# Norm transposes of a two-layer transformer kernel: from TensorE to transposing DMAs on SyncE's queue

## The chip, the cores and the metric

The kernel runs on one core of a Trainium2 chip. The metric is the device time of one launch in microseconds (us). The kernel before takes 1613.98 us, the median of three runs (1613.9 to 1615.33).

## The reference

The input x has 2048 rows of 512 bf16 values. Two layers follow, with the same weights in both:

```python
x = x + _A_ref(_layernorm(x, axis=-1), A_wqkv, A_wo)   # attention, 32 heads of 16
x = x + _B_ref(_layernorm(x, axis=-1), B_w1, B_w2)     # relu MLP, 512 -> 1792 -> 512
x = x + _A_ref(_layernorm(x, axis=-1), A_wqkv, A_wo)
x = x + _B_ref(_layernorm(x, axis=-1), B_w1, B_w2)
```

`_A_ref` makes q, k and v by one matmul, takes the softmax of q k^T / 4 over all 2048 keys, multiplies by v and by wo. `_layernorm` subtracts the mean and divides by the root of the variance plus 1e-5. So there are four norms over all 2048 rows, and the result of each is multiplied from the right by a weight matrix. The matmul contracts over partitions, so each normalised block of 128 rows x 512 columns has to be transposed to 512 x 128 first.

## The kernel before, in words

**Attention.** Scores are made transposed, keys on partitions and 512 queries along the free dimension, one PSUM bank for one head and one block of 128 keys. There are 4096 such banks. They are worked in *slots* of three banks (the `while units` loop from line 1173): TensorE makes the scores of a slot into one of two three-bank tiles `ps_s` (line 1302), ScalarE takes the exponential of two or three of them in one instruction (line 1311), and TensorE multiplies by the values and adds up in the bank `ps_o` (line 901). Four heads share TensorE by its four row groups.

**Pairs.** In about every second slot one of the three banks is handed to VectorE, which makes the exponential by a short chain: `lin` from the scores (line 995), and then, for two such banks together, `step` and `cube` (lines 1036 to 1051). Two banks together are a *pair*. A slot with one bank on VectorE has a shorter ScalarE instruction.

**The planner.** The order of instructions on each engine is written by the Python code itself, under a manual schedule. It keeps two model clocks, `now_pe` and `now_dve`, and gives each piece of work a cost in ns. `mark(key, engine, lag)` (line 240) records when a result is expected; `at(deps, engine)` (line 243) tells when an engine may use it. VectorE's tasks are in `dve_q`, with "musts" ahead (lin, and the copies that free a bank). A pair is started (lines 1196 to 1220) when fewer than four are in flight, when VectorE's expected backlog is under `BACKLOG`, and when its chain is expected to end before its segment does. In layer 0 no more than one pair at a time is in flight until the last value block is there (`("v", 0, 15)`).

**The filler.** All other matmuls (q, k, v, the output projection, the MLP) are "groups" in the lists `urgent` and `work`. They go through one PSUM bank, `ps_f`, one group at a time: TensorE fills the bank, VectorE empties it (`put_evac`, `do_evac`), and the next group may begin. `fill_pe` (line 307) puts pieces of them between the scores, as many as the ration `owed` allows; `pace` (line 1272) sets the ration per slot, 3.0 units of 216 ns in the first segments of layer 0. `fill_pe` takes the first group whose inputs are expected in time. `run_until` forces what is needed at once.

**The norms.** `ln_rows` (line 524) queues four steps: statistics of each block of 128 rows on VectorE (line 465), the inverse root on VectorE and GpSimd (lines 473 to 503, `RSTD_LAG` 5000 ns), the normalised block `xn` on VectorE (`ln_apply`, line 505), and then, as filler, `ln_groups` (line 549): four TensorE transposes of 128x128 into `ps_f` (`ln_transpose`, line 513) and one VectorE copy into `xnT` (line 558). A norm covers four row blocks, or two for the last four chunks of layer 1. `xnbuf` has one buffer for each of the four row blocks, so the apply of the next norm waits for the transpose of the one before (key `xT`). The key `xnT` releases the k, v, q and MLP groups.

The trace shows 64 row blocks: 58 through `ln_groups`, four in the opening code (lines 1090 to 1095) and two in the closing code (lines 1403 to 1406). These six are written out by hand.

**SyncE's queue.** It carries, in program order, the input loads at the start, the weight loads of the MLP (`load_w1`, line 662: one 128 KB block for each 128 hidden columns, four buffers), the stores of the output (line 711), and for the softmax sums two small DMAs per head group: line 828 spreads 512 sums over partitions so that VectorE's reciprocal (line 847) is short, line 848 brings them back. GpSimd's queue then broadcasts them (line 850). The planner expects 3600 ns for line 828 (`C_LAG`).

Of the kernel before, what the change touches and what calls it, by code (L numbers as in the profile page):

```python
# [24 lines left out]
def kernel(  # L25
# [10 lines left out]
    nc = tc.nc  # L36
    P = 128
# [12 lines left out]
    QS = 512  # L50
    NQS = S // QS
    TPC = QS // P
# [26 lines left out]
    C_LAG, R_LAG, U_LAG = 3600.0, 10500.0, 3000.0  # L79
    VLAG = 1  # L80
    RSTD_LAG = 5000.0
    AHEAD = (8.0, 8.0)
    LATE = 0.0
    MID = 2
# [15 lines left out]
    def sb(shape, dt, name):  # L100
        return persist.tile(shape, dt, name=name)
# [32 lines left out]
    xnT = [sb([P, NDC, QS], BF16, f"xnT{j}") for j in range(NQS)]  # L134
# [19 lines left out]
    xnbuf = [sb([P, D], BF16, f"xn{n}") for n in range(TPC)]  # L154
# [47 lines left out]
    def bank():  # L202
        if ending[0]:
            bank_no[0] += 1
            return (ps_f[:], ps_s[0][:, 0, :], ps_s[1][:, 0, :])[bank_no[0] % 3]
        if not wide[0]:
            return ps_f[:]
        n = bank_no[0] % 7
        bank_no[0] += 1
        in_bank[0] = (2, 0) if n == 6 else (n // W, n % W)  # L210
        if n == 6:
            return ps_f[:]
        return ps_s[n // W][:, n % W, :]
# [26 lines left out]
    def mark(key, engine="dve", lag=0.0):  # L240
        made[key] = (engine, (now_pe if engine == "pe" else now_dve)[0] + lag)
# [30 lines left out]
    work = []  # L272
# [5 lines left out]
    def task(cost, fn, makes=(), deps=(), place=None):  # L278
        t = {"cost": cost, "fn": fn, "makes": makes, "deps": deps}
        dve_q.insert(len(dve_q) if place is None else place, t)  # L280
        maker.update({k: t for k in makes})

    def group(pieces, makes, deps):
        g = {"pieces": pieces, "makes": makes, "deps": deps}
        maker.update({k: g for k in makes})
        return g

    def put_evac(cost, fn):
        evac.append((cost, now_pe[0] + PE_TO_DVE, fn))
# [160 lines left out]
    def columns(l, j):  # L450

        tt, n = chunks[l, j]
        return tt // TPC, tt % TPC * P, n * P
# [4 lines left out]
    def ln_n(tag):  # L458
        return ln_seq.index(tag) % 2

    def ln_stats(tag, tt, i):
        if tag not in ln_seq:
            ln_seq.append(tag)
        st = stats[i % 2]
        nc.vector.bn_stats(out=st[:], in_=x_t[tt][:])  # L465
        nc.vector.bn_aggr(out=mv[ln_n(tag)][:, i, :], in_=st[:])
# [38 lines left out]
    def ln_apply(tag, tt, i):  # L505
        n = ln_n(tag)
        nc.vector.tensor_scalar(
            out=xnbuf[i][:], in0=x_t[tt][:],
            scalar1=mv[n][:, i, 0:1], scalar2=ya_[n][:, i : i + 1],
            op0=ALU.subtract, op1=ALU.mult,  # L510
        )

    def ln_transpose(tag, i, b=None, at_bank=None):
        pt = (bank() if b is None else b).bitcast(BF16)
        for c in range(NDC):
            ins = nc.tensor.transpose(
                pt[:, c * P : (c + 1) * P], xnbuf[i][:, c * P : (c + 1) * P], ident[:]
            )
            if wide[0]:
                uses(ins, in_bank[0] if b is None else at_bank)  # L520
        mark(("xT", tag, i), "pe")
        return pt[:, 0 : NDC * P].rearrange("p (c f) -> p c f", c=NDC)

    def ln_rows(tag, tt, n, i):

        if tag not in ln_seq:
            ln_seq.append(tag)
        at_tag = ln_seq.index(tag)
        prev = ln_seq[at_tag - 1]
        rows_of_prev = chunks[prev[1:]][1]  # L530
        before_that = ln_seq[at_tag - 2] if at_tag > 1 else None
        old = each(chunks[before_that[1:]][1], "xn", before_that) if at_tag > 1 else []
        if ("st", tag, i) not in made:
            task(830, lambda: ln_stats(tag, tt + i, i), [("st", tag, i)], old)
        if i == n - 1:

            def rstd():
                ln_rstd(tag, 0)
                ln_newton(tag)
                mark(("rs", tag, 3), lag=RSTD_LAG)  # L540

            task(500, rstd, [("rs", tag, 3)], each(n, "st", tag) + old)
            for k in range(n):
                task(
                    325, lambda k=k: ln_apply(tag, tt + k, k), [("xn", tag, k)],
                    [("xT", prev, k)] * (k < rows_of_prev) + [("rs", tag, 3)],
                )

    def ln_groups(tag, dst, at_column, n, war):
        groups = []  # L550
        for i in range(n):

            def piece(i=i):
                pt = ln_transpose(tag, i)

                def fin():
                    a = at_column + i * P
                    nc.vector.tensor_copy(out=dst[:, :, a : a + P], in_=pt)
                    mark(("xnT", tag, i))

                put_evac(342, fin)

            groups.append(
                group([(1.3, piece)], [("xT", tag, i), ("xnT", tag, i)], [("xn", tag, i)] + war)
            )
        return groups

    def each(n, *key):
        return [key + (i,) for i in range(n)]
# [73 lines left out]
    def o_group(l, j, i):  # L643
        tt, n = chunks[l, j]
        a = columns(l, j)[1] + i * P

        def fin(b):
            nc.vector.tensor_add(out=x_t[tt + i][:], in0=x_t[tt + i][:], in1=b)
            mark(("o", l, j, i))
            ln_rows(("ln2", l, j), tt, n, i)  # L650

        return mm_group(
            [(ot[t][:, a : a + P], wo[:, t // 2, :]) for t in range(NT)], fin,
            [("o", l, j, i)],
            [("ot", l, j, t, i) for t in range(NT)],
        )
# [76 lines left out]
    def rest_of_chunk(l, j):  # L733

        b = before(l, j)
        xj, a, w = columns(l, j)
        n = w // P
        war_h = each(chunks[b][1], "z", *b) if b else []
        work[0:0] = [o_group(l, j, i) for i in range(n)] + ln_groups(
            ("ln2", l, j), xnT[xj], a, n, []  # L740
        )
        gs = [h_group(l, j, ft, war_h) for ft in range(0, NF, QS // w)]
        gs += [z_group(l, j, i) for i in range((l, j) == (1, LAST - 1), n)]
        if l == 0:
            gs += ln_groups(("ln1", 1, j), xnT[j], 0, TPC, [])
            gs.append(k_group(1, 0, j))
            gs += [v_group(1, kb) for kb in range(j * TPC, (j + 1) * TPC)]
            gs += [k_group(1, T, j) for T in range(1, 4)]
        return gs
# [321 lines left out]
    tag = ("ln1", 0, 0)  # L1071
    idle_matmuls(18)
    for e in range(2):
        nc.vector.tensor_reduce(
            out=mask[e][:],
            in_=ident[:].rearrange("p (g e d) -> p e g d", g=4, e=2)[:, e],
# [3 lines left out]
            out=qmask[e][:], in0=mask[e][:], scalar1=SCALE * LOG2E * UNIT, scalar2=None,  # L1080
# [9 lines left out]
    for i in range(TPC):  # L1090
        pt = ln_transpose(tag, i)
# [27 lines left out]
    for j in range(1, NQS):  # L1119
        tag = ("ln1", 0, j)  # L1120
        for i in range(TPC):
            ln_rows(tag, j * TPC, TPC, i)
        work.extend(k_group(0, T, 0) for T in FIRST_K[j])
        work.extend(ln_groups(tag, xnT[j], 0, TPC, []))
        work.append(k_group(0, 0, j))
        work.extend(v_group(0, kb) for kb in range(j * TPC, (j + 1) * TPC))
        if j == 1:
            work.extend(k_group(0, T, 1) for T in range(1, MID))
# [44 lines left out]
    while units:  # L1173
# [6 lines left out]
        for (sg, kb, g), *_ in banked:  # L1180
            if sg["n"] not in seen:
                seen.add(sg["n"])
                n = sg["n"] + 1
# [86 lines left out]
        if first["l"] and first["early"]:  # L1270
            rest = sum(x[0][0]["early"] for x in itertools.islice(units, 400)) / W - 20.0
        pace = (
            3.0 if first["short"] and not first["l"] else max(todo / max(rest + (-8.0 if first["j"] == NQS - 1 and not first["l"] else AHEAD[first["l"]] if first["j"] < (LAST if first["l"] else NQS - 1) else -6.0), 6.0), 0.5)
        )
# [34 lines left out]
        while len(pend) == NE:  # L1309
            force_v()  # L1310
        ex = nc.scalar.activation(  # L1311
            out=eb[:, 0 : place[m]], in_=b[:, 0 : place[m]], func=ACTF.Exp,
# [34 lines left out]
    l, j = 1, LAST  # L1347
    tag = ("ln2", l, j)
    tt, n_rows = chunks[l, j]
    rows = range(n_rows)  # L1350
    _, at_column, width = columns(l, j)
# [7 lines left out]
    def at_bank(b):  # L1359
        n, w = b  # L1360
        return ps_s[n][:, w, :] if n < 2 else (ps_f, ps_o)[n - 2][:]
# [41 lines left out]
    for i in rows:  # L1403
        pt = ln_transpose(tag, i, at_bank(more[i]), more[i])
# [4 lines left out]
    for ft in range(NF + 1):  # L1409
        if ft < NF:  # L1410
            n = (l * NQS + j) * NF + ft
# [6 lines left out]
            if ft % 2:  # L1418
                out = nc.scalar.activation(out=ht[ft][:, at_column : at_column + width], in_=at_bank(b)[:, 0:width], func=ACTF.Relu)
            else:  # L1420
                out = nc.vector.tensor_scalar(
                    out=ht[ft][:, at_column : at_column + width], in0=at_bank(b)[:, 0:width],
                    scalar1=0.0, scalar2=None, op0=ALU.max,
                )
# [8 lines left out]
    for i in rows:  # L1433
# [3 lines left out]
            out=out_flat[(tt + i) * P : (tt + i + 1) * P, :], in_=x_t[tt + i][:]  # L1437
# [31 lines left out]
```

The softmax here doesn't subtract the row's maximum and nothing guards it: scores larger than these inputs give would overflow.

## Time and profile before

| what | value |
|---|---|
| time, median of 3 | 1613.98 us |
| span of the profiled execution | 1611.5 us |
| ScalarE busy | 1566.0 us, 97% |
| VectorE busy | 1496.8 us, 93% |
| TensorE busy (matmul records) | 1451.6 us, 90% |
| 16 DMA engines, SyncE's hardware queue | 7.1% of their time |
| chain that ended last | 78% ScalarE, line 1311 |

Busy time is the union of the records of an engine; records of consecutive instructions overlap a little, so the spacing of starts is shorter than the mean duration. TensorE's records are pipelined, and 90% busy there is no 90% of its peak. The chain that ended last is followed back from the last instruction: its shares tell which engine's work the end hangs on. The waits name the instruction that came last before an engine went on. Entries such as SPq are instructions of a DMA queue; they show when a DMA was issued, and not when it landed.

### The profile page before, as it was taken

How to read it: one execution, taken by the hardware profiler on the slowest of the kernel's cores; microseconds unless marked ns; L12 is line 12 of the kernel's file. 1: busy time of each engine (PE TensorE's matmuls, PEld its weight loads, DVE VectorE, ACT ScalarE, POOL GpSimd, SP SyncE). 2: the span in 40 equal slices, each digit the busy share in tenths (PEclk: the TensorE clock that was granted, in tenths of full speed). 3: DMA queues.
4: the chain of work that ended last, by engine and by line, in shares of the span. 5: the costliest groups of instructions: out<-in, count | busy, mean ns of one | idle time of the engine just before them, and what ended most of it. 6: DMA issues, size and time to landing. Idle time of an engine off the chain costs nothing.

```text
span 1611.5 us, 35252 instructions
## 1 busy us (share of the span) xinstructions
PE 1451.6 (90%) x14667; PEld 508.9 (32%) x14863; DVE 1496.8 (93%) x3007; ACT 1566.0 (97%) x1387; POOL 93.8 (6%) x279
## 2 busy tenths in 40 slices
PE   8888888999989999899998998888989999899997
PEld 3222222322222222222222222222333333344444
DVE  7669999999999999999898998999999999999994
ACT  6999999999999999999999999999999999999993
POOL 2000001001010011000100000001001010010100
PEclk9999999999999999999999999999999999999999
DMA  5000000210002100021000100000210111121223
GB/s 164 1 1 2 2 2 10 46 28 12 5 18 45 21 15 9 12 47 25 9 1 17 31 1 1 2 3 9 44 30 16 26 29 36 22 48 36 47 46 73
DMA packets 113889, 39.97 MB, mean 25 GB/s; under 512 B 103328, under 2 KB 111264, under 8 KB 113728
## 3 DMA queue, kind: packets, MB, share of 16 engines
q1 hardware_dynamic: 101696, 26.21, 7.1%
q0 software_dynamic: 10688, 10.18, 3.4%
q8 instruction: 116, 1.90, 0.5%
q10 hardware_dynamic: 1344, 1.31, 0.2%
q14 instruction: 45, 0.37, 0.1%
HBM read 24.38 MB, written 2.10 MB: 16 GB/s over the span
## 4 chain that ended last, share of the span: by engine, by line
ACT 78%; PE 11%; DVE 7%; issue 3%; DMA 1%; ACTq 0%; DVEq 0%
ACT e L1311 78%; PE ps_s L1302 4%; PE ps_o L901 3%; PE ps_f L434 3%; DVE lin L995 2%; DVE step L1036 1%; PE ps_s L1365 1%; DVE cube L1047 1%; DVE cube L1051 1%; DVE stats L465 0%; DVE ht L682 0%; DVE q L625 0%; DVE ot L836 0%; DVE x L708 0%; DMA c<-u 0%
## 5 line engine op out<-in xcount | busy, mean ns | idle before, releaser
L1311 ACT ACTIVATE e<-ps_s 128x1024 bf16<-128x1024 f32 (+1 forms) x1366 | 1554.8, 1367 | 6.6 <-PE ps_s L1302 4.7
L1302 PE MATMUL ps_s<-q,ktp 32*128 32x512 bf16 (+1 forms) x6060 | 601.2, 341 | 106.7 <-ACT e L1311 84.7
L901 PE MATMUL ps_o<-e,vaug 128*32 128x512 bf16 (+1 forms) x4284 | 494.7, 345 | 11.3 <-DVE u L823 4.8
L995 DVE TENSOR_SCALAR lin<-ps_s 128x512 int16<-128x512 f32 x662 | 452.6, 686 | 35.8 <-PE ps_s L1302 30.4
L1302 PEld LDWEIGHTS <-ktp 32*128 32x128 bf16 x6060 | 189.9, 91 | 504.5 <-issue 375.6
L1036 DVE TENSOR_SCALAR step<-lin 128x1024 int16<-128x1024 int16 x662 | 262.9, 420 | 3.3 <-PE ps_o L901 0.6
L901 PEld LDWEIGHTS <-vaug 128*32 128x32 bf16 x6004 | 161.5, 94 | 302.2 <-issue 291.5
L1047 DVE TENSOR_TENSOR cube<-step 128x1024 f16<-128x1024 bf16 x331 | 225.9, 685 | 2.7
L1051 DVE TENSOR_TENSOR cube<-cube,lin 128x1024 bf16<-128x1024 f16 x331 | 225.5, 682 | 0.0
L901 PE MATMUL ps_o<-step,vaug 128*32 128x512 bf16 (+1 forms) x836 | 143.2, 340 | 0.3 <-issue 0.3
L901 PE MATMUL ps_o<-cube,vthird 128*32 128x512 bf16 (+1 forms) x788 | 138.2, 337 | 0.6 <-issue 0.3
L901 PE MATMUL ps_o<-lin,vaug 128*32 128x512 bf16 (+1 forms) x836 | 127.4, 338 | 4.1 <-DVE u L823 2.8
L434 PE MATMUL ps_f<-xnT,w 128*128 128x512 bf16 (+1 forms) x446 | 116.9, 345 | 5.6 <-issue 2.5
L434 PE MATMUL ps_f<-w,ht 128*128 128x512 bf16 x334 | 104.8, 384 | 5.6 <-issue 4.3
L850 POOL DMA_DIRECT2D r<-u x52 | 37.5, 721 | 1165.9 <-DVE step L1036 424.3
L434 PE MATMUL ps_f<-xnT,wqkv 128*128 128x512 bf16 (+1 forms) x288 | 82.3, 359 | 6.4 <-issue 2.5
L682 DVE TENSOR_SCALAR ht<-ps_f 128x512 bf16<-128x512 f32 x103 | 70.7, 687 | 3.2 <-PE ps_f L434 3.0
L434 PE MATMUL ps_f<-wo,ot 128*128 128x512 bf16 x206 | 65.4, 384 | 3.0 <-issue 1.9
L625 DVE TENSOR_SCALAR q<-ps_f,qmask 128x512 bf16<-128x512 f32 (+1 forms) x102 | 64.8, 661 | 3.1 <-PE ps_f L434 3.0
L434 PEld LDWEIGHTS <-w 128*128 128x128 bf16 x504 | 39.1, 97 | 60.0 <-issue 50.6
L836 DVE SCALAR_TENSOR_TENSOR ot<-u,mask,r 128x512 bf16<-128x512 f32 (+2 forms) x82 | 51.3, 627 | 1.1
L901 PEld LDWEIGHTS <-vthird 128*32 128x32 bf16 x788 | 39.8, 95 | 32.8 <-issue 30.1
(91 smaller groups left out, 609.8 us busy)
## 6 DMA issues: line engine op xcount, KB each, us to landing
w<-in_B_w_dram SPq DMA_DIRECT2D x140, 128.0 KB
r<-u POOLq DMA_DIRECT2D x25, 256.0 KB, 7.1
r<-u POOLq DMA_DIRECT2D x27, 128.0 KB, 4.5
out_dram<-x SPq DMA_DIRECT2D x16, 128.0 KB
x<-in_A_x_dram SPq DMA_DIRECT2D x14, 128.0 KB
w<-in_B_w_dram SPq DMA_DIRECT2D x1, 1792.0 KB
wqkv<-in_A_wqkv_dram ACTq DMA_DIRECT2D x2, 512.0 KB
c<-u SPq DMA_DIRECT2D x48, 8.0 KB
```

Of the source, the lines that this page charges most:

```text
L434: nc.tensor.matmul(out, lhsT, rhs, start=i % k == 0, stop=i % k == k - 1)
L625: return nc.vector.tensor_scalar(out=qbuf[n % 2][e][:, 0:w], in0=b, scalar1=qmask[e][:, 0:1], scalar2=None, op0=ALU.mult,)
L682: nc.vector.tensor_scalar(out=out, in0=sums, scalar1=0.0, scalar2=None, op0=ALU.max)
L836: nc.vector.scalar_tensor_tensor(out=ot[t][:, at_column + a : at_column + a + w], in0=u[:, a : a + w], scalar=mask[e][:, 0:1], in1=r[:, a ...
L850: nc.gpsimd.dma_start(out=r[:, 0:width], in_=bass.AP(tensor=sums.tensor, offset=sums.offset, ap=[list(sums.ap[0]), [0, 32], [1, width]],),)
L901: nc.tensor.matmul(ps_o[32 * g : 32 * g + 32, 0 : sg["w"]], values[:, 4 * sg["T"] + g, 2 * e : 2 * e + 32], rhs, start=g not in sg["begun" ...
L995: first = nc.vector.tensor_scalar(out=lin[which][:, half * QS : (half + 1) * QS], in0=src, scalar1=EXP_BIAS, scalar2=0.0, op0=ALU.add, op1 ...
L1036: nc.vector.tensor_scalar(out=stair, in0=line, scalar1=keep, scalar2=put, op0=ALU.bitwise_and, op1=ALU.bitwise_or,)
L1047: (609, lambda: nc.vector.tensor_mul(out=power, in0=mantissa, in1=mantissa)),
L1051: (609, lambda: nc.vector.tensor_mul(out=power.bitcast(BF16), in0=power, in1=line.bitcast(BF16))),
L1302: nc.tensor.matmul(b[:, a : a + sg["w"]], kt[32 * g : 32 * g + 32, kc : kc + P], qbuf[sg["n"] % 2][sg["e"]][32 * g : 32 * g + 32, 0 : sg[" ...
L1311: ex = nc.scalar.activation(out=eb[:, 0 : place[m]], in_=b[:, 0 : place[m]], func=ACTF.Exp, scale=1.0 / (LOG2E * UNIT),)
```

## The change

In place of the filler groups, each apply of a norm is followed at once by a transposing DMA on SyncE's queue, from `xn` to its columns of `xnT`. The aim is to take the transposes off TensorE, the one filler bank out of the path, and the copy off VectorE. The planner is told that the transposed block is there 4000 ns after the apply (`X_LAG`); the same moment frees `xn` for the next norm. The opening four row blocks and the closing two stay on TensorE.

```diff
+    X_LAG = 4000.0
...
             task(500, rstd, [("rs", tag, 3)], each(n, "st", tag) + old)
+            def apply(k):
+                kind, l, j = tag
+                xj, a, _ = columns(l, j) if kind == "ln2" else (j, 0, QS)
+                ln_apply(tag, tt + k, k)
+                a += k * P
+                nc.sync.dma_start_transpose(out=xnT[xj][:, :, a : a + P], in_=xnbuf[k][:])
+                mark(("xT", tag, k), lag=X_LAG)
+                mark(("xnT", tag, k), lag=X_LAG)
+
             for k in range(n):
                 task(
-                    325, lambda k=k: ln_apply(tag, tt + k, k), [("xn", tag, k)],
+                    325, lambda k=k: apply(k),
+                    [("xn", tag, k), ("xT", tag, k), ("xnT", tag, k)],
                     [("xT", prev, k)] * (k < rows_of_prev) + [("rs", tag, 3)],
                 )
-
-    def ln_groups(tag, dst, at_column, n, war):
-        groups = []
-        for i in range(n):
-
-            def piece(i=i):
-                pt = ln_transpose(tag, i)
-
-                def fin():
-                    a = at_column + i * P
-                    nc.vector.tensor_copy(out=dst[:, :, a : a + P], in_=pt)
-                    mark(("xnT", tag, i))
-
-                put_evac(342, fin)
-
-            groups.append(
-                group([(1.3, piece)], [("xT", tag, i), ("xnT", tag, i)], [("xn", tag, i)] + war)
-            )
-        return groups
...
-        work[0:0] = [o_group(l, j, i) for i in range(n)] + ln_groups(
-            ("ln2", l, j), xnT[xj], a, n, []
-        )
+        work[0:0] = [o_group(l, j, i) for i in range(n)]
...
-            gs += ln_groups(("ln1", 1, j), xnT[j], 0, TPC, [])
...
-        work.extend(ln_groups(tag, xnT[j], 0, TPC, []))
```

## The prediction

> **What bounds the kernel now.** I read the busy shares and costliest groups of the page first, then the waits, then the timeline of one norm, then the DMA queue of SyncE.
>
> From the page, parts 1 and 5, and the groups kept apart by form:
>
> ```profile
> PE 1451.6 (90%) x14667; PEld 508.9 (32%) x14863; DVE 1496.8 (93%) x3007; ACT 1566.0 (97%) x1387; POOL 93.8 (6%) x279
> ...
> L1311 ACT ACTIVATE e<-ps_s 128x1536 bf16<-128x1536 f32 x703 | 1052.1, 1573 | 4.5 <-PE ps_s L1302 2.8 <-PE ps_o L901 1.2
> L1311 ACT ACTIVATE e<-ps_s 128x1024 bf16<-128x1024 f32 x662 | 717.7, 1148 | 2.1 <-PE ps_s L1302 1.9 <-PE ps_o L901 0.2
> L995 DVE TENSOR_SCALAR lin<-ps_s 128x512 int16<-128x512 f32 x662 | 452.6, 686 | 35.8 <-PE ps_s L1302 30.4
> ...
> L558 DVE COPY xnT<-ps_f 128x512 bf16<-128x512 bf16 x58 | 24.3, 419 | 3.6 <-PE ps_f L516 3.2
> L507 DVE TENSOR_SCALAR xn<-x,mv,ya 128x512 bf16<-128x512 bf16 x64 | 23.1, 409 | 0.8 <-POOL ya L503 0.7
> L516 PE MATMUL ps_f<-ident,xn 128*128 128x128 bf16 x232 | 22.8, 221 | 2.0 <-DVE q L625 0.6 <-DVE xnT L558 0.5
> ```
>
> ScalarE does nothing but exponentials from 16.8 us to about 1578 us and is idle ahead of them for 6.6 us in all. The end is therefore a head of 17 us, the sum of the exponentials, and a tail of 34 us. The 4096 score banks (2 layers, 32 heads, 16 key blocks, 4 query strips) come in slots of three: 703 slots give ScalarE all three banks, 662 give one to VectorE. A bank taken from ScalarE shortens a slot by 1573 - 1148 = 425 ns. So the time is set by how many pairs of banks the planner can place on VectorE (now 331), and by whether ScalarE is ever kept waiting.
>
> VectorE is the second engine, and it is full: the stretches of the trace give it 273 of 280 us from 120 to 400, 388 of 400 from 400 to 800, 183 of 200 from 800 to 1000, 193 of 200 from 1000 to 1200, 347 of 360 from 1200 to 1560. From 20 to 120 us it has only 70 of 100 us of work, with 15 banks (0.15 per us, against 135 in 280 us, 0.48 per us, just after), because pairs are withheld until the last value block of layer 0 is there.
>
> One norm of layer 0, VectorE's timeline from 225 to 300 us:
>
> ```profile
> 273.00 1.37 DVE L507 TENSOR_SCALAR xn<-x,mv,ya 128x512 bf16<-128x512 bf16 x4
> ...
> 276.09 0.42 DVE L558 COPY xnT<-ps_f 128x512 bf16<-128x512 bf16 x1
> ...
> 282.50 0.42 DVE L558 COPY xnT<-ps_f 128x512 bf16<-128x512 bf16 x1
> ...
> 285.98 0.69 DVE L682 TENSOR_SCALAR ht<-ps_f 128x512 bf16<-128x512 f32 x1
> ```
>
> The four normalised row blocks are there at 274.4; the four transposes and copies, one at a time through the one filler bank, last until 282.9; the first MLP matmul on them starts at 283.05. This path is 8.5 us long.
>
> SyncE's queue and GpSimd at the same place:
>
> ```profile
> 277.04 0.54 SPq L848 DMA_DIRECT2D u<-c  x1
> ...
> 279.36 0.70 POOL L850 DMA_DIRECT2D r<-u  x1 [7.24 <-DVE step L1036]
> ```
>
> The GpSimd DMA at line 850 needs the bytes of the SyncE DMA at line 848: 2.32 us from issue to dependent (2.38 at 252.79 to 255.17). That is the price of a small DMA from SyncE here: 0.54 us of issue, about 2.3 us until a waiter goes on.
>
> **What the Trainium skill says.** "VectorE: DVE Perf Modes", section "The three transpose paths", gives a 128x128 bf16 transpose 390 ns on TensorE and 1309 ns by the DMA crossbar. The TensorE record here is 221 ns, so the table is above this trace; no DMA transpose is in it. "DMA: Bandwidth & Descriptors", section "Latency and other measured facts", gives a transposing DMA an effective 261 GB/s; no run shows it yet. The same page, section "Silent corruption: two transposing streams in flight at once", asks for waits between transposes of different queues; all of these are SyncE's, so none is added.
>
> **The change, part by part.**
>
> *VectorE.* It loses the 58 copies of line 558. A record is 419 ns, but records overlap; by the starts (35.52 to 35.86) one takes 0.34 us of the stream. A pair costs, by the same reading, 2 x 0.60 (lin) + 2 x 0.34 (step) + 2 x 0.61 (cube) = 3.10 us, and saves ScalarE 2 x 0.425 = 0.85 us. Twelve of the copies lie in 20 to 120 us, where VectorE has idle time anyway. The other 46 free 46 x 0.34 = 15.6 us, so 5.0 pairs, so 4.3 us of ScalarE.
>
> *TensorE and the filler bank.* 232 transposes go. TensorE is not what ends the waits of ScalarE, so these 22.8 us are worth nothing as such. But the filler is rationed: in the first segments of layer 0 it gets 3.0 units a slot. Twelve row blocks x 1.3 = 15.6 units, 5.2 slots less until the last value block; at 80 slots in 100 us that is 6.5 us earlier. In 6.5 us the pairs run at 0.48 in place of 0.15 banks per us: 2.1 banks, 0.9 us. Similar relief at the layer boundary I leave at zero.
>
> *The moved apply.* The 58 applies stay on VectorE. What follows is now 58 DMA instructions on SyncE, each waiting for its apply. Behind a waiting one stand the small DMAs of lines 828 and 848 and the weight loads of line 662. A reciprocal that waits for line 828 stops VectorE (now 0.2 us in all). Each transpose is emitted just behind its apply, so the queue waits about as long as VectorE's own order makes it, one slot at most, plus four issues: cost taken as zero, hidden by the planner's lag of 3.6 us against 2.3.
>
> *The new wait.* The first K or MLP matmul now waits for a DMA instead of a copy, and the planner believes in 4.0 us after the apply. TensorE is in order: a matmul that waits there holds the scores behind it. The cost of a transpose isn't in the trace, so I bound it. Low end: 128x512 bf16 is 131 KB, at 261 GB/s 0.50 us, and 2.3 us of fixed latency: 2.8 us. The four applies end 0.34 us apart, so the last is 1.0 us behind the first; the fourth transpose is issued 3 x 0.54 = 1.6 us behind the first, 0.6 us behind its own apply, and lands 3.4 us after it: inside the planned 4.0. High end: 1.31 us for every 128x128 block and no overlap, 5.2 us a row block, 21 us for four; with the 2.3 us the last lands some 22 us after the last apply. I take the low end, since 1.31 us for 32 KB reads like fixed cost and not like a rate. The path from apply to first matmul then shrinks from 8.5 to 4 or 5 us. With a score buffer ahead, TensorE has about one slot (1.1 us) before ScalarE notices, so a small lateness is hidden.
>
> Sum: 4.3 + 0.9 = 5.2 us less. 1613.98 - 5.2 = 1608.8 us.
>
> **The rivals.**
>
> *A: slightly late transposes (slower).* If a row block costs 1.3 us of the queue or the crossbar, the fourth lands 4 x 1.3 + 2.3 = 7.5 us after the first apply, 6.5 after the last; 2.5 us over the plan, 1.4 over what the score buffer hides. The 46 row blocks behind the head are 10 norms of four and 3 of two. 10 x 1.4 = 14 us of ScalarE idle, less the 5 gained: about 1623 us, and 1635 at 1.6 us a row block. For it: the 1309 ns figure. Against: the effective rate on the other page.
>
> *B: the crossbar is serial at 5.2 us a row block (much slower).* Beyond the plan and the buffer, 17 us in 10 norms and 7 us in 3: 10 x 17 + 3 x 7 = 191 us, so about 1800 us. VectorE's reciprocals would stop behind SyncE as well.
>
> *C: the freed time isn't turned into pairs (no change).* The planner starts a pair only when its backlog test, its due time and the pairs in flight allow; from 800 to 1000 VectorE already idles for 17 us. With a shifted order the plan may lose as much as it gains: 1612 to 1616 us.
>
> **How the numbers follow.** Forecast 0.62, A 0.18, B 0.07, C 0.13. The likeliest case gives 1608.8, and scatter of the planner's order puts it between 1602 and 1611. The range reaches up through C and most of A, to 1635, and leaves out the rest of A and all of B. Faster by over 0.2% (below 1610.8) 0.62; within 0.13; slower (above 1617.2) 0.25.
>
> **What would show it.** Right: lin of line 995 above 662 (some 675), the 1024-wide exponentials as many, the idle time ahead of line 1311 still under 10 us, more lin between 20 and 120 us, and transposes landing within 4 us. Wrong: TensorE at line 434 or its weight loads waiting for a DMA into xnT, with ScalarE idle behind it; or reciprocals at line 847 waiting for SyncE; or 662 lin unchanged. A transpose that holds SyncE for over 1.3 us would make the forecast wrong.

## The result, and the profile after

The changed kernel takes 1632.8 us (median of four runs, 1628.47 to 1637.48) against 1613.99 us before (1613.9 to 1615.33). The ratio is 1.0115, 95% interval 1.0084 to 1.0146. It is slower by 19 us; the forecast was 5 us faster.

The page of the kernel after, parts 1 and 3 (busy time of each engine; packets, MB and share of the DMA engines' time on two queues):

```profile
PE 1451.2 (89%) x14420; PEld 498.2 (31%) x14607; DVE 1491.8 (92%) x2965; ACT 1564.2 (96%) x1385; POOL 92.3 (6%) x279
...
q1 hardware_dynamic: 133248, 33.82, 10.1%
...
q8 instruction: 114, 1.87, 0.5%
```

No engine has become busier. ScalarE has 1.8 us less work in a span that is 17.5 us longer, so the loss is idle time. The groups of the kernel after, forms kept apart (busy us and mean ns of one, then the idle time ahead and what ended it), show where:

```profile
L1299 ACT ACTIVATE e<-ps_s 128x1536 bf16<-128x1536 f32 x697 | 1043.4, 1571 | 10.2 <-PE ps_s L1290 9.4 <-PE ps_o L890 0.7
L1299 ACT ACTIVATE e<-ps_s 128x1024 bf16<-128x1024 f32 x668 | 721.5, 1150 | 19.9 <-PE ps_s L1290 19.1 <-DVE step L1025 0.7
...
L984 DVE TENSOR_SCALAR lin<-ps_s 128x512 int16<-128x512 f32 x668 | 455.9, 686 | 50.5 <-PE ps_s L1290 45.5
...
L435 PE MATMUL ps_f<-xnT,w 128*128 128x512 bf16 x289 | 95.9, 393 | 17.6 <-DMA xnT<-xn 9.7 <-issue 2.5 <-DVE ht L674 2.1
L435 PE MATMUL ps_f<-xnT,wqkv 128*128 128x512 bf16 x232 | 75.5, 392 | 13.1 <-DMA xnT<-xn 7.2 <-issue 2.7 <-DVE vaug L603 0.9
```

The exponentials (line 1299, before line 1311) now wait 30.1 us in place of 6.6, nearly all of it for scores. The scores are late because TensorE stood at line 435, the MLP and K/V/Q matmuls, until a transposed block arrived. There are three pairs more than before (668 lin in place of 662), not five to seven. The waits of the kernel after, each with its total us, how often and the longest, say the same:

```profile
DVE lin L984 <- PE ps_s L1290: 45.5, 45, 7.6
...
ACT e L1299 <- PE ps_s L1290: 28.5, 29, 7.4
...
PE ps_f L435 <- DMA xnT<-xn: 17.0, 7, 6.9
...
DVE ot L825 <- DMA r<-u: 3.3, 3, 1.6
```

Seven waits of TensorE carry 17.0 us, up to 6.9 at a time. The view of the one line that issues the transposes (min, median and max ns for which one holds SyncE's queue, then who waited) gives the price that the trace of before could not show:

```profile
L549 SPq DMA_TRANSPOSE xnT<-xn x58: 1189/1220/3585, 28.2 to 1555.3; - x58
...
  PE ps_f L435: 17.0, 7
```

One transpose holds SyncE for 1.22 us, against 0.54 for the small softmax DMAs. From start to start in a row they are 1.31 us apart, and by the semaphores in the trace 39 of the 58 land 2.4 to 2.6 us after issue. Four in a row land 3 x 1.31 + 2.4 = 6.3 us after the first is issued. The other 19 land after 2.8 to 8.3 us. Beside nine of them a broadcast of GpSimd was in flight, and beside the other ten a 16 KB packet of the queue that the profile calls *instruction* (q8, about 1 us each).

The costliest wait, in the timeline of the kernel after from 664 to 684 us (start, duration, instruction, and in brackets the idle time before it and its releaser):

```profile
666.30 0.53 SPq L837 DMA_DIRECT2D u<-c  x1
...
666.88 3.04 SPq L549 DMA_TRANSPOSE xnT<-xn  x2
...
668.69 0.70 POOL L839 DMA_DIRECT2D r<-u  x1 [7.57 <-DVE step L1025]
...
676.59 1.44 PE L435 MATMUL ps_f<-xnT,w 128*128 128x512 bf16 x3 [6.88 <-DMA xnT<-xn]
...
677.97 0.61 PE L1290 MATMUL ps_s<-q,ktp 32*128 32x512 bf16 x3
...
678.62 1.02 ACT L1299 ACTIVATE e<-ps_s 128x1024 bf16<-128x1024 f32 x1 [7.45 <-PE ps_s L1290]
678.62 0.69 DVE L984 TENSOR_SCALAR lin<-ps_s 128x512 int16<-128x512 f32 x1 [7.63 <-PE ps_s L1290]
```

The fourth transpose of this norm went out at 668.71, 0.02 us after GpSimd's 256 KB broadcast of softmax sums. The broadcast landed at 676.12, the transpose at 676.5, 7.8 us after its issue. TensorE takes its instructions in order, so the scores at 677.97 stood behind the MLP matmul, and ScalarE and VectorE stood still for 7.5 us. The same place by stretches of 4 us (busy us of PE, PEld, DVE, ACT and POOL, granted TensorE clock, DMA share, GB/s):

```profile
668.00:672.00 4.00, 1.71 (x17) 0.49 (x14) 2.91 (x7) 3.17 (x3) 0.70 (x1) 1.00 0.62 82
672.00:676.00 4.00, 0.00 (x0) 0.00 (x0) 0.00 (x0) 0.00 (x0) 0.00 (x0) 0.60 0.24 50
676.00:680.00 4.00, 3.41 (x15) 0.63 (x15) 1.38 (x3) 1.02 (x1) 0.00 (x0) 0.50 0.00 0
```

For four microseconds no engine works, and afterwards TensorE has half its clock until 686.5. In the whole kernel the half clock covers 41.0 us in six stretches before the last exponential (before: 6.8 in two).

Of TensorE's seven waits for transposes, two fell beside a broadcast and make 10.3 of the 17.0 us (this one and 3.4 us at 599.4). Three fell after a transpose that an instruction packet had delayed (4.9 us, among them 2.1 at 798.4 and 2.2 at 867.8). In the last two nothing but the row of four was late (1.8 us).

The sum, from the two profiled executions (1611.5 and 1629.0 us): the exponentials start 0.1 us later; their records cover 1554.3 us in place of 1554.8; the gaps between them are 29.7 us in place of 6.2; the tail after the last one is 28.1 us in place of 33.7. That is 0.1 - 0.5 + 23.5 - 5.6 = +17.5 us. Of the 29.7 us of gaps, 19.5 lie in stretches of half clock.

### The profile page after: what moved, and what is told of

Same layout as the page of the kernel before. It is cut to its first block, busy times and chain, and to the rows that moved or that the text cites. A ratio compares the mean times of both kernels' runs of the same rounds, so it can differ in the third digit from the quotient of the medians.

```text
span 1629.0 us, 34843 instructions
## 1 busy us (share of the span) xinstructions
PE 1451.2 (89%) x14420; PEld 498.2 (31%) x14607; DVE 1491.8 (92%) x2965; ACT 1564.2 (96%) x1385; POOL 92.3 (6%) x279
## 3 DMA queue, kind: packets, MB, share of 16 engines
q10 hardware_dynamic: 1344, 1.31, 0.2%
## 4 chain that ended last, share of the span: by engine, by line
ACT 74%; PE 11%; DVE 9%; DMA 3%; issue 2%; POOL 0%; ACTq 0%; DVEq 0%; POOLq 0%
ACT e L1299 74%; PE ps_s L1290 4%; PE ps_f L435 3%; DVE lin L984 3%; PE ps_o L890 3%; DVE step L1025 1%; DMA r<-u 1%; DMA xnT<-xn 1%; DVE cube L1036 1%; DVE cube L1040 1%; PE ps_s L1353 1%; DVE stats L466 0%; DVE ht L674 0%; DVE ot L825 0%; DVE q L617 0%
## 5 line engine op out<-in xcount | busy, mean ns | idle before, releaser
L1299 ACT ACTIVATE e<-ps_s 128x1024 bf16<-128x1024 f32 (+1 forms) x1366 | 1554.3, 1364 | 30.1 <-PE ps_s L1290 28.5
L890 PE MATMUL ps_o<-e,vaug 128*32 128x512 bf16 (+1 forms) x4282 | 497.8, 347 | 13.7 <-DVE u L812 5.2
L1025 DVE TENSOR_SCALAR step<-lin 128x1024 int16<-128x1024 int16 x668 | 267.5, 421 | 5.6 <-PE ps_o L890 2.4
L435 PE MATMUL ps_f<-xnT,w 128*128 128x512 bf16 (+1 forms) x457 | 123.0, 349 | 18.6 <-DMA xnT<-xn 9.7
L435 PE MATMUL ps_f<-w,ht 128*128 128x512 bf16 x350 | 108.4, 383 | 6.5 <-issue 4.9
L435 PE MATMUL ps_f<-xnT,wqkv 128*128 128x512 bf16 (+1 forms) x296 | 86.0, 366 | 13.7 <-DMA xnT<-xn 7.2
```

The source lines that it names most:

```text
L435: nc.tensor.matmul(out, lhsT, rhs, start=i % k == 0, stop=i % k == k - 1)
L890: nc.tensor.matmul(ps_o[32 * g : 32 * g + 32, 0 : sg["w"]], values[:, 4 * sg["T"] + g, 2 * e : 2 * e + 32], rhs, start=g not in sg["begun" ...
L1025: nc.vector.tensor_scalar(out=stair, in0=line, scalar1=keep, scalar2=put, op0=ALU.bitwise_and, op1=ALU.bitwise_or,)
L1299: ex = nc.scalar.activation(out=eb[:, 0 : place[m]], in_=b[:, 0 : place[m]], func=ACTF.Exp, scale=1.0 / (LOG2E * UNIT),)
```

## The experiments

The first four runs (lag7, lag10, apart, dummy) set three theories against each other. **W**: TensorE waits in order for transposes that land later than the plan's 4.0 us. **T**: the extra traffic and SyncE's time for each transpose slow everything. **P**: the new order of work is slower by itself. A fourth, **Q**, narrows T and was put up after these runs: the transposes hold up the small softmax DMAs in SyncE's queue; VectorE then waits, with it TensorE and ScalarE. Under all of them the gain is small because the plan makes only three more pairs. Each time is a median, with the ratio to the kernel before on the same chip.

### lag7: tell the planner 7 us

```diff
-    X_LAG = 4000.0
+    X_LAG = 7000.0
```

> X_LAG from 4000 to 7000 ns, nothing else: the planner counts on a transposed block 7 us after its apply. Theory W (TensorE waits in order for transposes that land later than planned: four in a row need about 6.3 us, more beside a broadcast): waits of line 435 for xnT fall from 17 us to under 5, idle time ahead of the exponentials from 30 us to under 15, granted clock to 0.993 or more, time 1610 to 1617 us. Theory T (the extra traffic and SyncE's time per transpose slow everything): no change, 1627 to 1637 us. Theory P (the new order of work is worse by itself): above 1625 us with few waits for xnT.

Measured 1619.96 us, ratio 1.0033 (1.0019 to 1.0047). Its waits:

```profile
DVE ot L825 <- DMA r<-u: 6.5, 3, 3.2
...
PE ps_f L435 <- DMA xnT<-xn: 1.8, 2, 1.0
```

TensorE's wait for transposes falls from 17.0 to 1.8 us, and the excess over before from 1.15% to 0.33%. So the waits of theory W are a large part of the loss. They are not all of it: the time, the gaps (19.9 us) and the granted clock (0.988) each miss what W expected (1610 to 1617 us, under 15 us, 0.993 or more), and the half clock still covers 37.5 us. Of the 23.5 us of added gaps 13.7 remain; the net excess is smaller than that because the tail stays at 28.1 us. A part of what remains is VectorE's 6.5 us of waits for the broadcast sums, which later pointed to theory Q.

### lag10: tell it 10 us

The same edit with 10000.0.

> X_LAG from 4000 to 10000 ns, nothing else. Theory W: longer than the worst landing seen (8.3 us after issue), so no wait for xnT at all, idle ahead of the exponentials under 9 us, clock as before (0.996 or more); the plan holds 329 pairs, two fewer than before, 1.7 us: 1611 to 1619 us. Theory T: 1627 to 1637 us. Theory P: above 1625 us.

Measured 1626.93 us, ratio 1.0076 (1.0052 to 1.01), above the expected 1611 to 1619 and inside what theory P named (above 1625 us with few waits for transposes). Its waits for the sums' DMAs:

```profile
DVE r L849 <- DMA u<-c: 3.6, 1, 3.6
DVE ot L825 <- DMA r<-u: 3.5, 2, 2.2
DVE c L836 <- DMA c<-u: 3.3, 4, 0.9
```

No matmul waits for a transpose any more, yet the gaps are 17.9 us where under 9 were expected, and 10.4 us of VectorE's waits are for small DMAs. So W alone does not explain the loss. The plan also has only 329 pairs, five fewer than the kernel after. With the longer lag K, V and MLP groups, and the next norm's `xn`, are released later: the last value block of layer 0 is copied at 112.0 us in place of 96.7, and there are 15 lin from 20 to 120 us in place of 21. A longer expected delay is therefore no free insurance.

### apart: keep transposes and broadcasts apart

A norm's applies wait in the plan until a running broadcast should have landed; and a head group that ends near a norm spreads its sums by VectorE's own shuffle (`quick`), without GpSimd.

```diff
-                    [("xT", prev, k)] * (k < rows_of_prev) + [("rs", tag, 3)],
+                    [("xT", prev, k)] * (k < rows_of_prev) + [("rs", tag, 3), ("cast",)],
...
-        quick = sg["load"] is not None or ended[l, j] == NT
+        quick = sg["load"] is not None or ended[l, j] == NT or norm_near()
...
+            if not quick:
+                mark(("cast",), lag=R_LAG)
```

> X_LAG stays 4000 ns; the planner keeps transposes and GpSimd's broadcasts of the softmax sums apart (an apply waits until the last broadcast is expected to have landed; a segment that ends close to a norm spreads its sums on VectorE instead). Theory W with the broadcast as the main cause: the two long waits (3.4 and 6.9 us) go, idle ahead of the exponentials from 30 to 12 to 18 us, no landing over 4.5 us, 1612 to 1621 us. Theory W with the four transposes in series as the main cause: idle stays above 22 us, above 1624 us. Theory T: 1627 to 1637 us.

Measured 1618.37 us, ratio 1.0014 (0.9999 to 1.003). No transpose lands later than 4.43 us after its issue. Its waits:

```profile
DVE r L863 <- DMA u<-c: 7.5, 5, 2.7
...
PE ps_f L435 <- DMA xnT<-xn: 3.4, 5, 0.9
```

So the landings of over 4.5 us come with a broadcast in flight. The eleven that still take 3.1 to 4.4 us all have an instruction packet beside them. With the plan's 4.0 us unchanged the excess falls from 1.15% to 0.14%. The gaps, 19.2 us, lie between the 12 to 18 us expected with the broadcasts as the main cause and the 22 us expected with the row of four. The run also replaces nine of the 52 broadcasts by work on VectorE and plans 335 pairs, so the fall is not due to the collisions alone. The largest wait for a DMA that remains is again VectorE's, for a small SyncE DMA.

### dummy and dummy3: the kernel before, with transposes that nobody reads

To measure Q by itself, the kernel before keeps its TensorE transposes and also issues a transposing DMA behind each apply, to a spare buffer that nothing reads. The work of the kernel before is all there.

```diff
+    scrap = sb([P, NDC, P], BF16, "scrap")
...
+            def apply(k):
+                ln_apply(tag, tt + k, k)
+                nc.sync.dma_start_transpose(out=scrap[:], in_=xnbuf[k][:])
```

> The kernel before, with its TensorE transposes kept, and in addition the 58 transposing DMAs from the same xn blocks into a spare buffer that nobody reads; the plan and the order on the engines are those of before. Theory W: nobody waits for them, 1612 to 1617 us, as before. Theory T: the DMAs themselves cost, 1624 us or more. Theory P: as before.

All go to one buffer, so each waits for the one before to land, and a norm holds SyncE longer than in the kernel after. SyncE's timeline of dummy at the norm that the prediction showed (there the DMA `u<-c` went out at 277.04):

```profile
274.41 0.56 SPq L833 DMA_DIRECT2D c<-u  x1
275.03 9.41 SPq L546 DMA_TRANSPOSE scrap<-xn  x4
284.54 0.55 SPq L853 DMA_DIRECT2D u<-c  x1
```

and what stands behind it, in the timeline of all engines of dummy:

```profile
294.15 0.75 DVE L841 SCALAR_TENSOR_TENSOR ot<-u,mask,r 128x512 bf16<-128x512 f32 x1 [4.88 <-DMA r<-u]
...
296.76 0.61 PE L1307 MATMUL ps_s<-q,ktp 32*128 32x512 bf16 x3 [4.50 <-DVE lin L1000]
...
297.42 1.45 ACT L1316 ACTIVATE e<-ps_s 128x1536 bf16<-128x1536 f32 x1 [4.31 <-PE ps_s L1307]
```

Measured 1637.87 us, ratio 1.0135 (1.0111 to 1.0158), gaps 29.6 us, and no matmul reads a DMA's block. The sums leave SyncE 7.5 us late; the broadcast follows; VectorE's multiply waits 4.9 us, the lin behind it is late, TensorE waits for the bank that lin has to free, ScalarE for TensorE. The time is in the range of theory T, and the lines show by which way: SyncE's queue. That is theory Q, and W is not the only way to lose. How much depends on the hold, so dummy3 transposes only the first three blocks of a norm (`if k < 3:`):

> As the run with the 58 unread transposes beside the kernel before, but only the first three row blocks of each norm are transposed into the spare buffer. Each write to it waits for the one before, so SyncE was held for about 9.5 us a norm there; with three it is held for about 6.1 us, near the 5.2 to 5.6 us of the changed kernel. Theory Q (what costs is SyncE's queue: the small DMAs of the softmax sums stand behind the transposes, VectorE waits for them, TensorE for VectorE): 1619 to 1631 us. Theory W alone (only the waits for the transposed blocks cost): 1612 to 1617 us, as before.

Measured 1625.81 us, ratio 1.007 (1.0048 to 1.0091); the norm shown above now holds SyncE for 6.95 us, the gaps are 16.6 us. The waits of dummy3:

```profile
DVE ot L842 <- DMA r<-u: 4.7, 2, 2.4
...
DVE c L853 <- DMA c<-u: 3.2, 4, 2.2
```

Over the ten norms of four row blocks the median hold is 10.0 us in dummy (8.6 to 14.8) and 7.4 us in dummy3 (6.1 to 12.4), for 1.35% and 0.7%. In the kernel after it is 5.8 us (5.1 to 8.9), less than in either, so this is not the size of Q there; it shows that the term exists and grows with the hold. In the kernel after the waits of VectorE that show it directly are 3.3 us (`r<-u`), and no run isolates its whole size.

### model1 and queue2: count SyncE's queue in the plan

The planner gets a third clock. A transpose takes 1310 ns of it and lands 2200 (model1) or 2700 ns (queue2) after its turn; a small DMA takes 560 ns. model1 builds on apart, queue2 on the kernel after.

```diff
+    now_sp = [0.0]
+    def sp_issue(cost):
+        now_sp[0] = max(now_sp[0], now_dve[0]) + cost
+        return now_sp[0] - now_dve[0]
...
-                mark(("xnT", tag, k), lag=X_LAG)
+                lag = sp_issue(1310.0) + 2700.0
+                mark(("xnT", tag, k), lag=lag)
...
-                mark(("c", n), lag=C_LAG)
+                mark(("c", n), lag=sp_issue(560.0) + C_LAG - 560.0)
```

> The changed kernel with the planner told of both: broadcasts and transposes kept apart, and SyncE's queue counted (1310 ns for a transpose, 560 for a small DMA), so that a transposed block is expected 2.2 us after its turn in the queue and the sums' DMAs are expected later when they stand behind transposes. The plan holds 336 pairs. Theory Q and W together: idle time ahead of the exponentials under 12 us, waits of VectorE for the sums' DMAs under 3 us in all, 1608 to 1615 us. If the order of work itself is worse (theory P): above 1618 us.

> As the run with both told, but broadcasts and transposes are not kept apart, and a transposed block is expected 2.7 us after its turn in the queue. The plan holds 335 pairs. Theory: collisions with the broadcasts come back (landings of 6 to 8 us in a few norms), one or two waits of 3 to 7 us for xnT, 1613 to 1624 us; less than 1612 us would say that the broadcasts don't matter.

model1: 1613.11 us, ratio 0.9989 (0.998 to 0.9999); 336 pairs, gaps 12.0 us, half clock 13.7 us. queue2: 1613.67 us, ratio 0.9985 (0.9971 to 1.0); 335 pairs, gaps 12.3 us, half clock 17.1 us. The waits of model1:

```profile
DVE ot L844 <- DMA r<-u: 3.8, 1, 3.8
...
DVE r L871 <- DMA u<-c: 1.9, 1, 1.9
```

and one of queue2:

```profile
PE ps_f L435 <- DMA xnT<-xn: 4.2, 3, 2.4
```

With the true queue in the plan the net loss is gone, broadcasts kept apart or not. model1's waits for the sums' DMAs, 5.7 us, are above the 3 us expected. In queue2 a transpose still lands 8.55 us after issue beside a broadcast, which its plan doesn't count, yet TensorE waits only 4.2 us in all, less than expected. Each new plan is also another order of all the work, so how much is the count and how much the new order (theory P) no run tells. The forecast's 5 us don't come either: in the profiled execution of queue2 the exponentials are 3.3 us shorter than before and the tail 5.3, but the gaps are 6.1 us longer.

### split: two DMAs for each row block

queue2 with 256 columns to a DMA asks whether the 1.22 us belong to the bytes or to the instruction.

```diff
-                nc.sync.dma_start_transpose(out=xnT[xj][:, :, a : a + P], in_=xnbuf[k][:])
+                for h in range(2):
+                    nc.sync.dma_start_transpose(
+                        out=xnT[xj][:, 2 * h : 2 * h + 2, a : a + P],
+                        in_=xnbuf[k][:, 256 * h : 256 * h + 256],
+                    )
```

> The kernel with SyncE's queue counted in the plan (the plan unchanged), but each row block is transposed by two DMAs of 256 columns in place of one of 512. It tells what the 1.2 us for which a transpose holds SyncE is made of. If it is a cost per instruction: 1.2 us each, 2.4 us a row block. If it goes by size: 0.6 to 0.7 us each. A mixture, fixed part 0.5 us as for a plain small DMA: about 0.9 us each.

Its one timed execution took 1680.02 us. SyncE's timeline of split at one norm:

```profile
285.92 11.32 SPq L556 DMA_TRANSPOSE xnT<-xn  x8
297.33 0.55 SPq L848 DMA_DIRECT2D u<-c  x1
```

Eight DMAs of half the size hold the queue 11.3 us; each holds it 1.2 us and lands 2.4 us after issue, as the whole block did. From 512 columns downward the price is for the instruction. The gaps are 73.2 us in this execution: the plan still counts 1310 ns for a row block that now holds the queue twice as long.

### one4: one DMA for four row blocks

The other direction: queue2, where a norm of four blocks issues one transpose of 128 x 2048 behind its fourth apply, and the applies write the blocks interleaved. It computes something else than the reference, and where it departs from it was not followed up. Its transposes are read for their price alone.

```diff
+                elif k == n - 1:
+                    nc.sync.dma_start_transpose(
+                        out=xnT[xj][:].rearrange("p c (i r) -> p (c i) r", r=P), in_=xn_all[:]
+                    )
```

> queue2 with one transposing DMA for each norm of four row blocks (128 x 2048 in one instruction, issued behind the fourth apply) in place of four; the applies write their block interleaved so that one DMA covers them. The plan expects its landing 6.3 us after its turn; it has 335 pairs, as queue2. In the run with two DMAs per row block the hold of SyncE was 1.2 us for an instruction, whatever its size. Hold per instruction only: one transpose of four blocks holds SyncE some 1.2 to 2 us and lands within 4 us of its issue; reciprocals wait for SyncE's small DMAs under 2 us in all; time 1607 to 1613 us. Hold by size from 128 x 512 upward: about 4.9 us of hold and a landing some 6.5 us after issue, as four in series; waits as in queue2, 1611 to 1617 us.

SyncE's timeline of one4 at a norm with no broadcast beside it:

```profile
467.50 1.84 SPq L571 DMA_TRANSPOSE xnT<-xn_all  x1
```

Undisturbed, the large transposes hold SyncE 1.7 to 2.0 us, as here at 467.50, and land 4.2 to 4.4 us after issue, in place of 4 x 1.31 and 6.3 for four small ones. Beside a broadcast they still land after 7.5 to 9.6 us. The price is thus mostly per instruction upward as well: four times the bytes, some 1.5 times the hold. The time, 1624.31 us (ratio 1.0058, 1.0033 to 1.0083), is above the expectation: the waits of ScalarE for scores are 14.5 us, and the tail is 35.4 us against 28.4 in queue2.

### start12 and start12r: only where it pays

The kernel before, with transposing DMAs for the first norms of layer 0 only (12 row blocks), where SyncE carries nothing else that anyone waits for. start12 plans 4.0 us, start12r 5.0.

```diff
+            first = tag[:2] == ("ln1", 0)
+
+            def apply(k):
+                ln_apply(tag, tt + k, k)
+                if first:
+                    a = k * P
+                    nc.sync.dma_start_transpose(
+                        out=xnT[tag[2]][:, :, a : a + P], in_=xnbuf[k][:]
+                    )
...
-        work.extend(ln_groups(tag, xnT[j], 0, TPC, []))
```

> The kernel before with transposing DMAs for the first layer's first norm alone (12 row blocks, all before 60 us, where SyncE's queue carries no sums and GpSimd no broadcasts); all other norms on TensorE as before. The plan holds 334 pairs, three more. Theory Q and W: nothing waits, 3 x 0.85 us less than before: 1610 to 1615 us, faster than before by 0 to 0.3%. Theory P: no gain or slower.

> The kernel before with transposing DMAs for the first 12 row blocks alone, once more with more rounds; X_LAG 5000 in place of 4000 ns, which leaves the planned number of pairs at 334. Expected as in the first run of it: 1608 to 1613 us, 0.1 to 0.3% faster than before.

start12: 1610.69 us, ratio 0.9981 (0.9966 to 0.9996). start12r: 1610.27 us (1607.82 to 1613.82), ratio 0.9977 (0.9968 to 0.9985). It is faster than both kernels. lin of start12r from 20 to 120 us (busy us and count, clock, DMA share, GB/s):

```profile
20.00:120.00 100.00, 14.41 (x21) 1.00 0.13 28
```

There are 21 lin in place of the 15 of the kernel before, three pairs, and 668 in all: as many as in the kernel after, with gaps of 5.9 us. All twelve transposes land within 2.6 us of their issue. So the change's whole gain in pairs comes from these 12 row blocks.

## Why the prediction was wrong, point by point

**What bounds the kernel** was read rightly. ScalarE sets the end, and the prediction's own line was that its idle time stay under 10 us; it is 30.1.

**The new wait: this step failed, in its spacing and in taking the landing as fixed.** Undisturbed, the landing was near: 2.8 us were put, 2.4 measured. But the fourth transpose was put 3 x 0.54 us behind the first, with the issue time of a small plain DMA. It is 3 x 1.31. The fourth lands 6.3 us after the first's issue where the plan allows about 5.0 (the fourth apply ends 1.0 us behind the first, plus 4.0). That makes every norm of four late by some 1.3 us even undisturbed. By itself this made two of TensorE's seven waits, 1.8 of 17.0 us. The second part was not in the prediction at all: 2.3 us was the latency of a small DMA with nothing beside it. The small DMAs of the sums are followed by a GpSimd broadcast, and a transpose in flight beside it lands up to 7.8 and 8.3 us after issue (two waits, 10.3 us); beside an instruction packet it lands after 2.8 to 4.2 us (three waits, 4.9 us). lag7 and apart, which each remove lateness in another way and with another plan, take away 0.8 and 1.0 of the 1.15 points.

**The moved apply: "cost taken as zero" failed.** It named the right victims, lines 828 and 848, and then gave them no time, with the same 0.54. A norm of four holds the queue for 5.1 to 8.9 us. dummy and dummy3 show that holding it costs time without any reader of a transpose; with the queue and the landing counted in the plan, in queue2, the net loss is gone.

**VectorE's freed time: 4.3 us that didn't come.** The freed 15.6 us were turned into five pairs by dividing. After 120 us there is no pair more: 647 lin start there in both kernels. This is the plan's doing and not the chip's: the code itself places 334 pairs, before 331. A count in the plan after the last value block of layer 0, of which condition of lines 1196 to 1220 refuses a pair, gives "four in flight" 273 times, no segment with room for the chain 33 times, and VectorE's backlog never; in the kernel after 272 times, 38 times and never. That is rival C's mechanism, shown for the plan alone. A fifth buffer for lin would test it on the chip, but does not fit in SBUF beside the rest; it wasn't tried.

**The head: right, and too small.** The prediction put the last value block 6.5 us earlier, and 2.1 banks, 0.9 us, on that. The copies of the value blocks between 20 and 120 us, before and after (min, median and max ns, first and last start):

```profile
L611 DVE CAST vaug<-ps_f x14: 680/692/693, 19.9 to 111.2; 128x512 bf16<-128x512 f32 x14
L603 DVE CAST vaug<-ps_f x14: 681/692/693, 20.1 to 96.7; 128x512 bf16<-128x512 f32 x14
```

The last one is 14.5 us earlier. At the prediction's own rates, 0.48 in place of 0.15, that gives 4.8 banks. Six came, here and in start12: 6 x 0.425 = 2.6 us. start12 confirms it: its exponentials cover 2.7 us less, and its time is 0.19% or 3.1 us less.

**The tail** was left out. It is 28.1 us in place of 33.7. Before, two relu instructions and the last addition of an MLP chunk ran after the last exponential (1579.3 to 1583.9); now they are done by then. The kernels that send the later norms by one DMA a row block (after, lag7, lag10, apart, model1, queue2) have tails of 28.1 to 30.5 us; before, dummy, dummy3, start12 and start12r have 33.4 to 33.9. The filler bank, relieved of its groups near the end, is a possible reason. It is not enough by itself: one4 sends its last norms in the same way and has 35.4 us, with four relu instructions after the last exponential. The cause stays open.

**Rival A**, at 0.18, had the price and the place of the wait. "1.3 us of the queue for a row block" is what was measured. But its 14 us of ScalarE idle time were ten equal waits of 1.4 us; there were 23.5 us, and the row of four alone accounts for 1.8 us of TensorE's waits. That its 1623 us lies nearest to the measured time is in part luck, and the stated range holds that time only because it was stretched over A. Missing were the broadcasts, SyncE's other customers, and the clock: two thirds of ScalarE's gaps lie in half-clock stretches. "TensorE: Matmul & The Clock Gate" of the Trainium skill, section "Part 1: The HAM clock gate", gives half rate after an idle window of 3413 ns. The stretches here are one to four times 3.41 us long, which agrees. But they also follow TensorE gaps of 2.1 and 2.2 us (at 798.4 and 867.8 us), and one of 1.1, shorter than a window, and one stretch (from 993.7) follows no gap over 1 us.

What the clock costs can be estimated from the spread of one kernel's executions. In the 33 executions of the kernel before that ran beside lag7, the span rises from 1609.0 to 1617.1 us while the granted clock falls from 1.000 to 0.992. That is 0.31 us for each us at half clock (correlation 0.99); the 20 of lag7 give 0.34. At 0.3, the 34.2 us more of half clock in the kernel after would be an estimated 10 of its 17.5 us. This is a correlation: a stop brings the half clock along with its own wait, and no run separates the two.

**The choice between the bounds.** The low end was taken because 1309 ns for 32 KB "reads like fixed cost and not like a rate". That is right; the conclusion was not. A fixed cost of one instruction is paid 58 times on the queue that issues it. It belonged in the spacing of the four transposes, and there it gives rival A.

## What to carry to other kernels

Price a DMA by two numbers: how long it holds the queue that issues it, and when it lands. The first delays all that stands behind it on that queue, and a late small DMA can stop three engines in turn. Where a schedule is written out by hand, give the queue a clock of its own before moving work to it, and move first only what lies where the queue is empty: 12 of the 58 transposes brought the pairs, the other 46 all but 0.8 us of TensorE's waits for them. And measure a landing beside the DMAs that will be in flight with it: 2.4 us alone were up to 8.3 beside a broadcast.

## What the runs showed of the hardware that was not expected

- A transposing DMA of 128 x 512 bf16 from SBUF to SBUF holds SyncE 1.22 us and lands 2.4 us after issue; with 256 columns it is the same, with 2048 some 1.9 and 4.3 us. A plain weight load of 128 KB holds it 0.37 us where nothing is in its way. "Advanced Engine Details and Errata" of the Trainium skill, section "X-Bar Transpose (TRN2)", has transposes as fast as regular DMAs; for the landing this is near (by the same semaphores 2.3 us, the median of the weight loads), for the hold it is not.
- In a row that is 131 KB every 1.31 us, 100 GB/s. The 261 GB/s of "DMA: Bandwidth & Descriptors", section "Latency and other measured facts", are not reached in this size.
- Beside a 256 KB broadcast of GpSimd, which itself takes 7.1 us to land, the two slowest transposes landed 0.4 and 2.2 us after the broadcast did, 7.8 and 8.3 us after issue, and one held SyncE 3.6 us.
- Apart from the transposes of one4, every landing of over 2.6 us, in all runs, had a broadcast or a 16 KB packet of the instruction queue in flight beside it. With such a packet alone 88 landed 2.6 to 4.5 us after issue, and 26 as if nothing were there.
- Each of the 20 stops of TensorE of over 2.0 us (2.06 to 6.88), in the 13 profiled executions, has a stretch of 3.4 us or more at half clock that begins at most 1.6 us after the stop's end. After stops of 1 to 2 us it comes in some cases and not in others, and 21 of the 64 stretches before the last exponential begin without a stop of over 1 us, so the stop is not the only way to it.
